# A v cast behind its masks and attention rows ahead of a gate selection, in one TensorE-bound kernel

## The chip, the cores and the metric

The kernel runs on one core of a Trainium2 chip. The metric is the time of one execution on the device in microseconds; lower is better. The core has five engines with an instruction queue each: TensorE (PE in the profile, its weight loads PEld), VectorE (DVE), ScalarE (ACT), GpSimd (POOL) and SyncE (SP), which here only issues transfers. Each engine takes its instructions in the order in which they were written, and waits where an operand or a buffer isn't ready.

## What is computed

The reference is a block-sparse attention followed by a Fourier mixing layer with a small feed-forward network. Cut to what matters:

```
# q, k, v: batch 4, heads 8, seq 768, head dim 64; blocks of 64 keys, 12 of them
gate = einsum(q, mean of k over each block)      # per query and block; future blocks -1e9
sel  = top 3 blocks of the gate, and the query's own block
attn = softmax(where(sel and causal, q k^T / 8, -1e9))
x    = attn @ v                                  # heads side by side: 4 x 768 x 512
u    = x + real(fft(fft(x, axis=seq), axis=model))
un   = (u - mean(u)) / sqrt(var(u) + 1e-6)
out  = u + relu(un @ w_ch1) @ w_ch2              # 512 -> 2048 -> 512
```

## The kernel before

The heads are taken in pairs, four pairs to a batch, so there are 16 pairs, numbered from 0. The whole program is one list of steps written out by hand, ORDER (L115). Each entry is a step's name and its arguments; WORK (L862) says which function it calls. A step appends its instructions to the queues of the engines that it uses, so an engine's order is the order of ORDER restricted to the steps that use it. There is no planner.

The steps that play a part here, P being a pair, i one of six score tiles, b a batch:

- Gate: g:P (TensorE, L414) gate scores in PSUM; gt:P (VectorE, L431) turns them into gt; gx:P (L445) takes the largest eight of each row; gl:P,0 sets the own block's entry and gl:P,1 (L453) compares gt with the third largest, which writes lt: this comparison is a VectorE operation on two SBUF tensors; gm:P (L472) turns lt back into the mask mt. qs:P (GpSimd, L404) copies the queries q32 as float16 into qk, kh:P (GpSimd, L368) is a small product with the block means.
- Scores: s:P,i (TensorE, L487), e:P,i (ScalarE exponential into pt, L515), d:P,i (GpSimd, L523), the causal mask on the diagonal of tile i.
- Values: vc:P (GpSimd, L316) casts the loaded v (nat) to float16 in v16, one of four buffers; v:P (TensorE, L529) is 42 matmuls av that need every tile pt of the pair, its masks, and v16; x:P (VectorE, L542) is a reciprocal rcp of the row sums and one multiplication of av, in PSUM, that writes the rows x of the pair. It also frees the PSUM bank of av.
- Fourier mixing of a batch: fs and fd (VectorE folds of x, L556 and L566, each on two SBUF tensors), f (four more folds, fg), fc (GpSimd, four edge copies, the tile mid among them), y (TensorE), ty:b,0 (ScalarE) and ty:b,1 (here VectorE) copy it out of PSUM, tr:b,0 and tr:b,1 (VectorE, L626) write it reversed, m (TensorE, L632, mx in the profile) is the second transform, u (VectorE, L682) adds x, nm and xu (ScalarE) scale the rows, xt (TensorE) and un (VectorE) turn them.
- Feed-forward: w and r, then c and o; W and X load the weights through GpSimd's queue.

PSUM is handed out in four slots in an order written out by hand as well (PLACES, L187). A slot is given to a new tile only when the last reader of its old tile is done: so the scores s:3,3 take the slot of the av of pair 1, which x:1 empties.

The two places are these. At about 32 us VectorE has the half gl:4,1 of pair 4's selection and behind it x:1, while TensorE works on pair 3's scores. At about 48 us GpSimd has vc:4 (the fifth pair's cast), then the masks d:4,1, the product kh:6, and the masks d:4,4 and d:5,0; behind them qs:6. At that time VectorE does ty:0,1, tr:0,0, tr:0,1 and the sums u of batch 0, and TensorE the steps m of batch 0, then v:4.

Of the kernel before, what the change touches and what calls it, by code (L numbers as in the profile page):

```python
# [120 lines left out]
d:0,1 v:0 ks:3 kh:4 kc:4 Lq:5 kh:3 kc:3 s:1,3 x:0 qs:3 tq:4 e:1,3 d:1,4 s:2,2 d:1,2 qc:4 d:1,3 g:3  # L121
e:2,2 fs:0,1 s:1,5 s:2,1 gt:3 vc:1 e:1,5 s:2,5 Lv:2 e:2,1 g:4 gx:3 qs:4 s:2,0 gl:3,0 e:2,5 gl:3,1
d:1,5 e:2,0 tk:5 gt:4 d:1,1 Lv:3 d:2,2 gx:4 s:2,3 LT:0 d:1,0 s:2,4 Lq:6 gm:3 e:2,3 d:2,5 d:2,1 ks:5
tq:5 e:2,4 v:1 qc:5 kh:5 d:2,0 kc:5 d:2,3 Lk:6 gl:4,0 fs:0,0 s:3,2 gl:4,1 qs:5 x:1 s:3,4 e:3,2 g:5
d:2,4 vc:2 e:3,4 gt:5 s:3,3 s:3,0 gx:5 vc:3 LF:0 e:3,0 s:3,5 v:2 gm:4 fs:1,0 e:3,5 gl:5,0 d:3,4
e:3,3 gl:5,1 d:3,5 s:3,1 x:2 d:3,2 Lv:4 s:4,1 d:3,0 e:3,1 s:4,2 d:3,3 Lq:7 fs:2,0 s:4,3 e:4,1 fs:2,1
gm:5 d:3,1 v:3 W:1 fs:1,1 e:4,3 fd:2,1 fd:2,0 s:4,5 e:4,2 s:5,2 x:3 e:5,2 s:4,0 fs:3,1 s:5,0 fs:3,0
e:4,5 s:5,1 fd:3,1 e:4,0 tk:6 fd:3,0 fc:0 e:5,0 f:0,1 s:4,4 f:0,0 Lk:8 e:5,1 ks:6 y:0,0,0 d:4,5
e:4,4 d:4,0 y:0,0,1 f:0,2 f:0,3 y:0,1,0 d:4,2 ty:0,0 y:0,1,1 d:5,2 d:4,3 kc:6 s:5,3 ty:0,1 d:5,1
s:5,4 W:0 e:5,3 m:0,0 tr:0,0 tr:0,1 e:5,4 m:0,2 vc:4 u:0,0 u:0,1 nm:0,0,1 d:4,1 s:5,5 xu:0,0 m:0,1  # L130
kh:6 u:0,4 d:4,4 nm:0,1,1 e:5,5 d:5,0 u:0,5 nm:0,4,1 xt:0,0 xu:0,1 tq:6 Lk:7 u:0,2 nm:0,5,1 xu:0,4
xt:0,1 u:0,3 v:4 nm:0,2,1 xu:0,5 qc:6 xu:0,2 xt:0,4 un:0,0 xt:0,5 nm:0,3,1 qs:6 xu:0,3 g:6 un:0,2
d:5,4 xt:0,2 xt:0,3 W:2 gt:6 w:0,6,2 w:0,6,0 un:0,1 d:5,3 w:0,5,2 d:5,5 gx:6 w:0,5,0 w:0,5,1 gl:6,0
gl:6,1 gm:6 w:0,6,1 r:0,5 x:4 w:0,3 r:0,6 Lv:5 s:6,3 r:0,3 Lq:8 s:6,2 e:6,3 s:6,4 tq:7 s:6,1 e:6,4
# [780 lines left out]
```

## Time and profile before

| what | value |
|---|---|
| median of 3 runs | 283.35 us (283.18 to 283.54) |
| profiled execution | 283.3 us |
| its span, first to last instruction | 281.6 us |
| TensorE, VectorE, ScalarE, GpSimd busy | 97%, 67%, 60%, 44% of the span |
| granted TensorE clock | 1.00 throughout |

A row of a timeline has the start in microseconds from the start of the span, the length, the engine, the line of the kernel, the operation, what it writes and reads (out<-in, without buffer numbers), their sizes, and how many alike were merged into the row; in brackets stands how long the engine sat idle ahead of it and who ended that. A row of the waits has the waiting instruction, whom it waited for, the sum, the count and the longest. A row by stretches has the bounds, the length, then the busy time and the instruction count of PE, PEld, DVE, ACT and POOL, the granted clock, and the share and rate of the DMA engines. A row of a tile's instructions has the count, the shortest, median and longest duration in ns, and the first and last start in us. Lines such as L246 and L249 are helpers that several steps share, so steps are told apart by their tiles.

### The profile page before, as it was taken

How to read it: one execution, taken by the hardware profiler on the slowest of the kernel's cores; microseconds unless marked ns; L12 is line 12 of the kernel's file. 1: busy time of each engine (PE TensorE's matmuls, PEld its weight loads, DVE VectorE, ACT ScalarE, POOL GpSimd, SP SyncE). 2: the span in 40 equal slices, each digit the busy share in tenths (PEclk: the TensorE clock that was granted, in tenths of full speed). 3: DMA queues.
4: the chain of work that ended last, by engine and by line, in shares of the span. 5: the costliest groups of instructions: out<-in, count | busy, mean ns of one | idle time of the engine just before them, and what ended most of it. 6: DMA issues, size and time to landing. Idle time of an engine off the chain costs nothing. (4 is left out here: it accounts for less than half of the span.)

```text
span 281.6 us, 6726 instructions
## 1 busy us (share of the span) xinstructions
PE 272.2 (97%) x2577; PEld 168.8 (60%) x2577; DVE 187.5 (67%) x570; ACT 168.3 (60%) x230; POOL 122.9 (44%) x318
## 2 busy tenths in 40 slices
PE   7899899999999999999999999999999999999995
PEld 3666676776556655565666654566676545665544
DVE  2888998997977888998379875862184463514114
ACT  3698799769694396595735789659651631353000
POOL 2258748314796459636803873855602020002000
PEclk9999999999999999999999999999999999999999
DMA  8999999997789998749895084440000352400104
GB/s 177 237 210 214 253 171 180 188 165 125 133 115 190 168 123 176 143 87 233 183 150 99 3 249 102 116 134 3 0 3 0 136 147 56 151 0 0 40 37 149
DMA packets 120020, 35.55 MB, mean 126 GB/s; under 512 B 110834, under 2 KB 116018, under 8 KB 119988
## 3 DMA queue, kind: packets, MB, share of 16 engines
q1 hardware_dynamic: 114260, 29.48, 52.6%
q0 software_dynamic: 3984, 5.24, 11.2%
q10 hardware_dynamic: 1744, 0.40, 0.8%
q8 instruction: 20, 0.33, 0.5%
q14 instruction: 12, 0.10, 0.1%
HBM read 29.60 MB, written 7.34 MB: 131 GB/s over the span
## 5 line engine op out<-in xcount | busy, mean ns | idle before, releaser
L520 ACT ACTIVATE pt<-sc 128x1024 f16<-128x1024 f32 (+1 forms) x96 | 82.9, 934 | 24.4 <-PE sc L503 19.7
L756 PE MATMUL h<-unT,w 128*128 128x256 f16 (+1 forms) x528 | 87.0, 321 | 0.0
L781 PE MATMUL c<-w_sb,hT 128*128 128x512 f16 x368 | 83.2, 379 | 0.0
L756 PEld LDWEIGHTS <-w 128*128 128x128 f16 x528 | 51.0, 98 | 31.3
L781 PEld LDWEIGHTS <-hT 128*128 128x128 f16 x368 | 35.7, 98 | 40.7 <-issue 0.5
L766 ACT ACTIVATE hT<-h 128x768 f16<-128x768 f32 x48 | 37.7, 819 | 36.1 <-PE h L756 36.1
L526 POOL TENSOR_SCALAR_AFFINE_SELECT pt<-pt 128x256 f16<-128x256 f16 x96 | 37.6, 416 | 23.8 <-ACT pt L520 22.4
L764 DVE TENSOR_SCALAR hT<-h 128x768 f16<-128x768 f32 x16 | 15.1, 947 | 28.2 <-PE h L756 28.2
L793 DVE SCALAR_TENSOR_TENSOR u<-c,rs,u 128x512 f32<-128x512 f32 (+2 forms) x26 | 17.7, 701 | 24.0 <-PE c L781 22.7
L249 POOL TENSOR_SCALAR_AFFINE_SELECT qk<-q 64x768 f16<-64x768 f32 (+1 forms) x25 | 20.8, 831 | 19.1 <-DVE q L402 7.3
L249 POOL TENSOR_SCALAR_AFFINE_SELECT qk<-mt 32x160 f16<-32x160 f16 x72 | 23.0, 340 | 10.1 <-DVE mt L475 6.9
L503 PE MATMUL sc<-qk 96*128 96x512 f16 (+3 forms) x144 | 26.7, 306 | 0.0
L538 PEld LDWEIGHTS <-pt 128*128 128x128 f16 x672 | 22.2, 97 | 2.7 <-issue 0.7
L538 PE MATMUL av<-v,pt 128*128 128x65 f16 x672 | 23.2, 193 | 0.5 <-POOL v L249 0.4
L503 PEld LDWEIGHTS <-qk 96*128 96x128 f16 x144 | 12.8, 98 | 8.1 <-issue 0.5
L246 POOL TENSOR_TENSOR t<-vr,rs 128x6 f32<-128x6 f32 x12 | 2.6, 218 | 32.1 <-DVE rs L732 31.4
L701 ACT ACTIVATE x<-u,nm 128x512 f16<-128x512 f32 x24 | 16.4, 714 | 0.3
L721 DVE BATCH_NORM_STATS2 bst<-u 128x6 f32<-128x512 f32 x24 | 16.2, 677 | 0.1
L498 PE MATMUL sc<-qk 64*128 64x512 f16 (+3 forms) x112 | 14.8, 306 | 1.4 <-DVE x L246 0.8
L246 DVE TENSOR_TENSOR x<-av,rcp 128x768 f16<-128x768 f32 x16 | 15.3, 958 | 0.5
L687 DVE SCALAR_TENSOR_TENSOR u<-mx,x 128x512 f32<-128x512 f32 x20 | 12.8, 678 | 3.4 <-DMA out_dram<-u 2.2
L387 ACT CAST qk<-k 64x768 f16<-64x768 f32 x18 | 14.9, 828 | 0.2
(112 smaller groups left out, 319.6 us busy)
## 6 DMA issues: line engine op xcount, KB each, us to landing
nat<-in_v_dram SPq DMA_DIRECT2D x16, 384.0 KB, 4.9
out_dram<-u SPq DMA_DIRECT2D x23, 256.0 KB, 2.1
nat<-in_k_dram SPq DMA_DIRECT2D x38, 96.0 KB, 4.1
nat<-in_q_dram SPq DMA_DIRECT2D x38, 96.0 KB, 3.8
nat<-in_k_dram SPq DMA_DIRECT2D x12, 192.0 KB, 4.3
nat<-in_q_dram SPq DMA_DIRECT2D x12, 192.0 KB, 4.5
w_sb<-in_moe_w_ch_dram POOLq DMA_DIRECT2D x2, 1024.0 KB, 11.7
w<-in_moe_w_ch_dram POOLq DMA_DIRECT2D x2, 768.0 KB, 7.3
```

Source lines behind the costliest of these rows:

```text
L246: (eng or nc.vector).tensor_tensor(out=out, in0=in0, in1=in1, op=op)
L249: nc.gpsimd.affine_select(out=out, in_=in_, pattern=[[0, i] for i in n], base=0, channel_multiplier=0, compare_op=ALU.is_ge, fill=0.0)
L503: nc.tensor.matmul(ps[:, e, co:co + q1 - q0], qk[0:96, e, 1, 128 * jt:128 * jt + 128], qk[0:96, e, 0, q0:q1], start=True, stop=True)
L520: nc.scalar.activation(out=d["pt"][:, o:o + 2 * n].rearrange("p (e c) -> p e c", e=2), in_=d["sc", i][:, :, 0:n], func=AF.Exp, scale=0.125)
L526: nc.gpsimd.affine_select(out=dg, in_=dg, pattern=[[0, 2], [1, 128]], base=0, channel_multiplier=-1, compare_op=ALU.is_ge, fill=0.0)
L538: nc.tensor.matmul(av[:, e, 66 * st:66 * st + 65], pt[:, co:co + 128], vv[:, e, jt, 0:65], start=(cnt == 0), stop=(cnt == 20))
L701: nc.scalar.activation(out=x_t[b][:, kt, :], in_=u_t[b, kp][:, k2, :], func=AF.Identity, scale=0.0625, bias=u_t[b, kp, "m"][:, k2:k2 + 1])
L721: nc.vector.bn_stats(out=bst, in_=u_t[b, kt // 2][:, kt % 2, :])
L756: nc.tensor.matmul(hp[:, l:r], w1s, unT[:, dt, l:r], start=(dt == 0), stop=(dt == NDT - 1))
L766: nc.scalar.activation(out=hT, in_=hp, func=AF.Relu)
L781: nc.tensor.matmul(c_ps[b, g[0]][:, st - g[0], :], h_t[b, it][:, 128 * st:128 * (st + 1)], w2_t[0][:, it, :], start=(it == 0), stop=(it == ...
L793: nc.vector.scalar_tensor_tensor(out=o, in0=ps, scalar=st_t[b][1][:, st:st + 1], in1=o, op0=ALU.mult, op1=ALU.add)
```

## The change

Two entries of ORDER stand elsewhere; the work is the same. x:1 stands ahead of gl:4,1, so that VectorE does the reciprocal and the rows of the second pair first and the comparison for the fifth pair's gate after them; GpSimd's qs:5, which stood between the two, follows both and is on another engine. vc:4 stands behind d:5,0 and ahead of u:0,5, so that GpSimd does d:4,1, kh:6, d:4,4 and d:5,0 first. The other changed line is only broken elsewhere.

```
-tq:5 e:2,4 v:1 qc:5 kh:5 d:2,0 kc:5 d:2,3 Lk:6 gl:4,0 fs:0,0 s:3,2 gl:4,1 qs:5 x:1 s:3,4 e:3,2 g:5
+tq:5 e:2,4 v:1 qc:5 kh:5 d:2,0 kc:5 d:2,3 Lk:6 gl:4,0 fs:0,0 s:3,2 x:1 gl:4,1 qs:5 s:3,4 e:3,2 g:5
...
-s:5,4 W:0 e:5,3 m:0,0 tr:0,0 tr:0,1 e:5,4 m:0,2 vc:4 u:0,0 u:0,1 nm:0,0,1 d:4,1 s:5,5 xu:0,0 m:0,1
-kh:6 u:0,4 d:4,4 nm:0,1,1 e:5,5 d:5,0 u:0,5 nm:0,4,1 xt:0,0 xu:0,1 tq:6 Lk:7 u:0,2 nm:0,5,1 xu:0,4
+s:5,4 W:0 e:5,3 m:0,0 tr:0,0 tr:0,1 e:5,4 m:0,2 u:0,0 u:0,1 nm:0,0,1 d:4,1 s:5,5 xu:0,0 m:0,1 kh:6
+u:0,4 d:4,4 nm:0,1,1 e:5,5 d:5,0 vc:4 u:0,5 nm:0,4,1 xt:0,0 xu:0,1 tq:6 Lk:7 u:0,2 nm:0,5,1 xu:0,4
```

## The prediction

> **What bounds the kernel now.** I read the page first, then busy time by stretches, then TensorE's own waits, then the timelines around the two moved steps. Both clocks of the argument are in the profile of one execution: 283.3 us, of which 281.6 are the span, so 1.7 us lie around it; the median of the runs is 283.35, that is 0.05 more.
>
> ```profile
> span 281.6 us, 6726 instructions
> PE 272.2 (97%) x2577; PEld 168.8 (60%) x2577; DVE 187.5 (67%) x570; ACT 168.3 (60%) x230; POOL 122.9 (44%) x318
> PE 21%; DVE 0%; issue 0%
> ...
> 30.00:50.00 20.00, 17.81 (x323) 13.25 (x321) 18.49 (x46) 18.16 (x22) 14.07 (x30) 1.00 1.12 197
> 50.00:220.00 170.00, 169.37 (x1577) 106.50 (x1578) 125.57 (x391) 113.34 (x155) 90.22 (x231) 1.00 0.66 119
> ...
> PE sc L498 <- DVE x L246: 0.8, 1, 0.8
> PE mx L641 <- DVE tr L629: 0.7, 1, 0.7
> PE av L538 <- POOL v L249: 0.4, 1, 0.4
> PE yp L608 <- POOL mid L594: 0.2, 1, 0.2
> ```
>
> TensorE is busy 97% of the span at a granted clock of 1.00. The chain that ended last is TensorE alone and reaches back only through the last 21%, so it says nothing about the middle; the two stretches do. From 50 to 220 us the first column after the length, TensorE, is busy 169.37 of 170.00 us: whatever reaches 50 us earlier can end earlier, as nothing there waits for a fixed time. From 30 to 50 us it is busy 17.81 of 20.00, and VectorE (18.49) and ScalarE (18.16) are as full. The waits name the holes: 0.8 us for attention rows x and 0.7 us for the turned tile tr lie in that stretch. These are the two places that the change touches.
>
> **The second pair's rows, x:1.** It goes from behind gl:4,1 (the second half of a gate selection, one comparison into lt) to ahead of it. Nothing is added or removed, and no DMA is passed on any queue.
>
> ```profile
> 30.44 1.44 PE L538 MATMUL av<-v,pt 128*128 128x65 f16 x42
> 32.73 0.69 PE L421 MATMUL g<-q,kr 128*32 128x288 f32 x8
> 34.24 0.39 PE L498 MATMUL sc<-qk 64*128 64x384 f16 x4 [0.81 <-DVE x L246]
> 44.18 0.76 PE L608 MATMUL yp<-fs_sb,fg 128*128 128x193 f16 x7 [0.20 <-POOL mid L594]
> ...
> 32.16 0.89 DVE L246 TENSOR_TENSOR lt<-gt,mx 128x108 f16<-128x108 f32 x1
> 32.97 0.22 DVE L549 RECIPROCAL rcp<-av 128x12 f32<-128x12 f32 x1
> 33.22 0.96 DVE L246 TENSOR_TENSOR x<-av,rcp 128x768 f16<-128x768 f32 x1
> 34.09 0.47 DVE L435 STREAM_TRANSPOSE gt<-g 128x288 f32<-128x288 f32 x1
> 36.15 0.27 DVE L246 TENSOR_TENSOR lt<-gt,mx 128x108 f16<-128x108 f32 x1
> 36.70 0.23 DVE L549 RECIPROCAL rcp<-av 128x12 f32<-128x12 f32 x1 [0.28 <-PE av L538]
> 44.87 1.22 DVE L246 TENSOR_TENSOR fg<-zw 128x762 f16<-128x762 f16 x2
> ...
> 36.70:46.09 9.39, 8.75 (x155) 6.90 (x154) 9.18 (x19) 9.39 (x12) 5.75 (x14) 1.00 1.11 175
> ...
> 31.98 0.94 POOL L249 TENSOR_SCALAR_AFFINE_SELECT qk<-q 128x768 f16<-128x768 f32 x1
> 33.27 1.75 POOL L249 TENSOR_SCALAR_AFFINE_SELECT v<-nat 128x768 f16<-128x768 f32 x2
> 36.59 1.48 POOL L526 TENSOR_SCALAR_AFFINE_SELECT pt<-pt 128x256 f16<-128x256 f16 x4 [1.21 <-ACT pt L520]
> ...
> 32.52 1.94 ACT L520 ACTIVATE pt<-sc 128x1024 f16<-128x1024 f32 x2 [0.52 <-PE sc L510]
> 35.22 10.74 ACT L520 ACTIVATE pt<-sc 128x1024 f16<-128x1024 f32 x13 [0.76 <-PE sc L510]
> ```
>
> The comparison takes 0.27 us at 36.15 and 0.89 us at 32.16, where it ends 0.13 us behind GpSimd's 0.94 us copy of the queries: it stood still while that copy ran. The rows x took their 0.96 us at 33.22 beside GpSimd's casts of v, so they don't stand still. Their input av was ready at 30.44 + 1.44 = 31.88, before the comparison began. So x:1 can take the comparison's place: reciprocal at 32.16, rows at 32.41, end 33.37 in place of 34.18, a shift of 0.81. TensorE's scores at 34.24 wait for the PSUM bank that x empties; the matmuls ahead of them end at 32.73 + 0.69 = 33.42, so almost all of the 0.81 us hole closes.
>
> That is not yet the gain, since the stretch that follows is VectorE's: 9.18 us busy of 9.39 from 36.70 to the last fold at 46.09, in order, and TensorE waits for its folds at 44.18. What arrives there early waits there longer. VectorE's own list begins with gt at 34.09, behind both steps. The comparison, now last, comes up at 32.41 + (34.09 - 33.22) = 33.28, just when the first cast of v begins (33.27). If it stands still until that cast ends, half of 1.75 us later, and ends 0.13 us after, it is done at 34.27 and gt starts some 0.1 us later than now. But behind it VectorE idled 0.28 us at 36.70, for the av of the third pair, which TensorE now delivers early. Net: 0.28 - 0.10, some 0.2 us gained. One bound: the comparison slips in before the cast, gt starts at about 33.5, and x:2 is held only by TensorE, whose last scores ahead of av need a bank that ScalarE's two exponentials free at 32.52 + 1.94 = 34.46; with some 0.2 us of scores and 1.44 for av x:2 can start near 36.2, a gain of 0.5. The other bound: ScalarE, idle 0.76 us at 35.22 for scores, runs that much earlier, so GpSimd's four selects of 36.59 begin at about 35.8 and may stop two VectorE operations between two SBUF tensors there, a select of 0.37 each: 2 x 0.37 - 0.2, a loss of 0.55. I take a gain of 0.2, because the 0.28 us idle row is the nearest measurement of slack on VectorE.
>
> **The fifth pair's v cast, vc:4.** On GpSimd it goes from ahead of d:4,1, kh:6, d:4,4 and d:5,0 (three masks and a small product) to behind them. The queue keeps its work and passes no DMA: W:0 is issued ahead, as before, and qs:6 comes last.
>
> ```profile
> 47.82 0.91 POOL L249 TENSOR_SCALAR_AFFINE_SELECT v<-nat 128x768 f16<-128x768 f32 x1
> 48.68 0.41 POOL L526 TENSOR_SCALAR_AFFINE_SELECT pt<-pt 128x256 f16<-128x256 f16 x1
> 49.05 0.23 POOL L246 TENSOR_TENSOR kr<-kr,half 128x24 f32<-128x24 f32 x1
> 49.24 1.00 POOL L526 TENSOR_SCALAR_AFFINE_SELECT pt<-pt 128x256 f16<-128x256 f16 x2
> 54.59 0.83 POOL L249 TENSOR_SCALAR_AFFINE_SELECT qk<-q 128x768 f16<-128x768 f32 x1 [4.34 <-DVE q L402]
> ...
> 47.88 2.11 DVE L629 COPY tr<-ty 128x768 f16<-128x768 f16 x2
> L629 DVE COPY tr<-ty x2: 553/1094/1635, 47.9 to 49.4; 128x768 f16<-128x768 f16 x2
> L629 DVE COPY tr<-ty x2: 362/362/363, 98.7 to 99.8; 128x768 f16<-128x768 f16 x2
> 49.91 0.68 DVE L687 SCALAR_TENSOR_TENSOR u<-mx,x 128x512 f32<-128x512 f32 x1
> ...
> 48.60 0.27 PE L642 MATMUL mx<-fd_sb,ty 128*128 128x256 f16 x1
> 49.57 0.28 PE L641 MATMUL mx<-fd_sb,tr 128*128 128x256 f16 x1 [0.70 <-DVE tr L629]
> 50.05 0.28 PE L641 MATMUL mx<-fd_sb,tr 128*128 128x256 f16 x1
> 53.00 1.45 PE L538 MATMUL av<-v,pt 128*128 128x65 f16 x42
> ```
>
> The third row of the second part is the next batch: a copy tr takes 362 ns there. Here the first took 1635 ns and the second 553. The first started at 47.88, just behind the cast, stood through the cast, a mask and the product, and ended at 47.88 + 1.64 = 49.51, 0.27 us after the next mask began (49.24); the second ended at 49.99. TensorE lost 0.70 us at 49.57 and again until 50.05, and VectorE's sums u could only start at 49.91.
>
> From the starts above, GpSimd's steps are 0.86 us apart for the cast, 0.37 for a mask, 0.19 for the product. The new queue is then d:4,1 at 47.82, kh:6 at 48.19, d:4,4 at 48.38, d:5,0 at 48.75, vc:4 from 49.12 to 49.98. The first tr again starts at 47.88. I let it be passed over until the product has gone, as in the row: it ends at 48.38 + 0.27 = 48.65. The mask d:4,4 is held up meanwhile (the two last masks took 1.00 us, against 0.41 + 0.37, so about 0.11 each) and makes way at 48.38 + 0.11 + 0.37 = 48.86; the second tr, 0.25 us later like its row, ends at 49.11. Against 49.99 that is 0.88 us. TensorE is free for it: its eighth ty matmul starts at 48.60. VectorE's u, which starts beside GpSimd in both orders and took its 0.68 us there, moves up by the same amount.
>
> Bounds. If tr gets in behind the first mask it ends at 48.19 + 0.27 = 48.46 and the second around 48.76; TensorE then bounds it: the ty matmuls give way at 48.71, the first two of tr take 0.22, so the row of 50.05 comes at 48.93, a gain of 1.12. If it is passed over three times, as often as now when the cast is counted, it ends at 48.75 + 0.27 = 49.02, and the second behind d:5,0 at about 49.5: a gain of 0.49. I take 0.88, as it follows the row's own step, the product. The cast itself is hidden: it ends at 49.98, v:4 needs it at 53.00 less what is gained, some 52.0, and d:4,1 to d:5,0, now early, have no one waiting. Without those 2 us each microsecond of delay would be one of TensorE's.
>
> The Trainium skill, on the page "SBUF — State Buffer", section "SBUF: two separate sides", calls the access that VectorE and GpSimd share an exclusive lock: who starts first keeps it for its whole instruction, and the other one blocks. Read strictly it lets the copy in after one instruction, and the sum would then be 283.3 - 1.12 - 0.2 = 282.0; the 1635 ns row disagrees, since the copy there outlasted three. The same rule speaks against the other move, as it puts the comparison against the cast of v at 33.27 for the whole cast.
>
> **Sum.** 283.3 - 0.88 - 0.2 = 282.2 for the profiled execution, 282.3 with the 0.05 to the median.
>
> **The rivals.** First, x:1 gives nothing back to the end, or takes a little, because VectorE meets the earlier selects in one place (0.37 - 0.2, so 0.2 lost): 283.35 - 0.88 + 0.2 = 282.7. For it: TensorE's early arrival can only wait at 44.18. Against: the 0.28 us idle is there to be used.
> Second, absorbed later: TensorE has waited 0.4 us for a v cast behind 50 us (the third wait above); if GpSimd or a transfer there doesn't move up with the rest, TensorE waits longer at it and about 283.2 is left. For it: that wait itself; against: it is the only one in 170 us.
> Third, slower: VectorE doesn't get in at all while GpSimd has another instruction ready. The new run from 47.82 to 49.98 is unbroken; then the first tr ends near 50.25, the second near 50.6, 0.6 late; likewise the comparison at 33.28 stands through both casts until 35.02 and ends at 35.15, so gt is 1.0 late, 0.7 behind the idle time. 283.35 + 0.6 + 0.7 = 284.7. It decides from the point where the second tr ends past 49.99. Against: tr got in at 49.24 and the comparison at 32.92 between instructions that followed each other.
> Fourth, the 1635 ns don't come from GpSimd at all, and the move changes nothing there: 283.1, x:1 alone.
>
> **How the numbers follow.** A change of under 0.2%, 0.57 us, can't be told from none here. The forecast, both parts paying, has 0.65, from 281.7 (1.12 + 0.5) to 282.8; 0.62 of it lies beyond 0.2%. The first rival has 0.14, its time just faster: 0.09 faster, 0.05 within. The second has 0.09, within. The third 0.08, slower. The fourth 0.04, within. That makes 0.71 faster, 0.21 within, 0.08 slower. The range goes from 281.7 to 283.4, the sum of the worst ends of both parts (0.49 gained, 0.55 lost), and leaves out the third rival and some of the tails.
>
> **What would show it.** Right: x ends at 33.4, the scores behind it without a wait; lt at about 33.3 takes near 1 us; x:2's reciprocal starts at 36.5; in the mx stage, counted from the start of GpSimd's W:0, the first tr ends 1.6 us later, not 2.5, and TensorE's 0.70 us wait shrinks below 0.2. Wrong: a tr over 1.6 us, an lt over 1.7 us, a longer TensorE wait for folds at 44 us that eats everything, or a new wait past 50 us.

## The result

The changed kernel takes 283.82 us (median of 22 runs), the kernel before 283.24 us beside it (22 runs): a ratio of 1.0024, with a 95% interval from 1.0016 to 1.0033. It is slower by about 0.6 us, where some 1.1 us less (0.88 and 0.2) was forecast, and lies above the range.

TensorE's waits in the changed kernel, by the waiting line, its releaser, the sum in us, the count and the longest:

```profile
span 282.8 us, 6727 instructions
...
PE mx L641 <- DVE tr L629: 1.3, 1, 1.3
PE tp L346 <- DMA nat<-in_q_dram: 0.6, 1, 0.6
PE tp L350 <- DMA nat<-in_k_dram: 0.6, 1, 0.6
PE yp L608 <- POOL mid L594: 0.6, 1, 0.6
PE av L538 <- POOL v L249: 0.4, 1, 0.4
PE sc L498 <- DVE x L246: 0.4, 2, 0.2
PE av L538 <- DVE gt L436: 0.2, 1, 0.2
```

The 0.8 us ahead of the scores is gone, as forecast. In its place stand two waits for x and one for gt of some 0.2 us each, and the wait for the folds (mid) grew from 0.2 to 0.6. The wait for tr, which was to shrink below 0.2, grew from 0.7 to 1.3. Behind that stage no new wait came; the 0.4 us for a cast of v stands there as before.

The same timelines as in the prediction, now of the changed kernel:

```profile
32.33 0.45 DVE L246 TENSOR_TENSOR sd<-x 128x384 f16<-128x384 f16 x1
32.96 0.96 DVE L246 TENSOR_TENSOR x<-av,rcp 128x768 f16<-128x768 f32 x1
33.83 0.97 DVE L246 TENSOR_TENSOR lt<-gt,mx 128x108 f16<-128x108 f32 x1
34.91 0.48 DVE L435 STREAM_TRANSPOSE gt<-g 128x288 f32<-128x288 f32 x1
37.25 0.22 DVE L549 RECIPROCAL rcp<-av 128x12 f32<-128x12 f32 x1
38.50 0.83 DVE L246 TENSOR_TENSOR sd<-x 128x384 f16<-128x384 f16 x2
...
33.79 1.78 POOL L249 TENSOR_SCALAR_AFFINE_SELECT v<-nat 128x768 f16<-128x768 f32 x2
38.64 0.49 POOL L526 TENSOR_SCALAR_AFFINE_SELECT pt<-pt 128x256 f16<-128x256 f16 x1 [0.68 <-ACT pt L520]
47.77 0.79 POOL L848 DMA_DIRECT2D w<-in_moe_w_ch_dram  x1
48.58 0.42 POOL L526 TENSOR_SCALAR_AFFINE_SELECT pt<-pt 128x256 f16<-128x256 f16 x1
48.95 0.24 POOL L246 TENSOR_TENSOR kr<-kr,half 128x24 f32<-128x24 f32 x1
49.15 0.90 POOL L526 TENSOR_SCALAR_AFFINE_SELECT pt<-pt 128x256 f16<-128x256 f16 x2
50.01 0.89 POOL L249 TENSOR_SCALAR_AFFINE_SELECT v<-nat 128x768 f16<-128x768 f32 x1
...
L629 DVE COPY tr<-ty x2: 799/1284/1770, 48.6 to 49.3; 128x768 f16<-128x768 f16 x2
```

Part of the 1.2 us between the two spans is not the change's. The first row, a fold sd ahead of both moved steps, starts at 32.33 against 31.79 before: this execution was 0.54 us late before it reached them, after waits for the first transfers of q and k. That start differs from one execution to the next (30.8 to 32.3 us in the profiles of this document). So the stretches are compared from marks within each execution: from that sd row to the start of GpSimd's W:0 (the weight load at 47.77) for x:1, and from there to the end of the span for vc:4. The marks of the kernel before are these two rows:

```profile
31.79 0.45 DVE L246 TENSOR_TENSOR sd<-x 128x384 f16<-128x384 f16 x1
47.02 0.79 POOL L848 DMA_DIRECT2D w<-in_moe_w_ch_dram  x1
```

| kernel | sd | W:0 | span | sd to W:0 | W:0 to end |
|---|---|---|---|---|---|
| before | 31.79 | 47.02 | 281.6 | 15.23 | 234.6 |
| changed | 32.33 | 47.77 | 282.8 | 15.44 | 235.0 |

By these marks x:1 cost 0.2 us and vc:4 0.4 us. Together that is the 0.6 us of the medians. Each is read from one execution; the table behind the experiments shows how well such marks repeat.

### The profile page after: what moved, and what is told of

It reads as the page before. It is cut to its first block, busy times and chain, and to the rows that moved or that the text cites. A ratio compares the mean times of both kernels' runs of the same rounds, so it can differ in the third digit from the quotient of the medians.

```text
span 282.8 us, 6727 instructions
## 1 busy us (share of the span) xinstructions
PE 272.7 (96%) x2577; PEld 169.2 (60%) x2577; DVE 188.3 (67%) x570; ACT 168.2 (60%) x230; POOL 123.3 (44%) x318
```

## The experiments

The theory at this point: VectorE operations that stand still beside GpSimd explain both parts. The second copy tr is kept out by the whole rest of GpSimd's run, the cast at its end included, and the comparison and a fold take back what x:1 won. The rivals: all of it is x:1's; it is the early transfers; the copies tr are slow for another reason than GpSimd. Each row of the table at the end of this section comes from the profile of the kernel named. Four kernels (tail_short, product_last, tail_product and cast_twice) ran once only, so nothing is read from their times.

**The cast alone** (cast_only):

```
-... m:0,2 vc:4 u:0,0 u:0,1 nm:0,0,1 d:4,1 ... kh:6 u:0,4 d:4,4 ... d:5,0 u:0,5
+... m:0,2 u:0,0 u:0,1 nm:0,0,1 d:4,1 ... kh:6 u:0,4 d:4,4 ... d:5,0 vc:4 u:0,5
```

> Only vc:4 is moved, x:1 stands as before. Theory (the copies tr are kept out while GpSimd's instructions follow each other without a gap, so the cast at the end of the run prolongs the wait): the second tr again outlasts the cast, 1.6 to 1.8 us, ends some 3.3 us behind the start of W:0 in place of 2.97 before, TensorE waits about 1.2 us for tr, and the time is 0.3 to 0.5 us over before. Rival one (the loss comes from x:1 ahead of the gate selection, and the cast is neutral or gains): within 0.2 us of before, or up to 0.9 us under it. Rival two (the loss is the transfers at 10 us, which came later in the profile of the changed kernel): no difference to before beyond the noise.

Its ratio to before is 0.9997 (0.9981 to 1.0013), medians 283.52 and 283.34: the interval holds both a loss of 0.36 us and none. The profile is sharper; the instructions on tr, with shortest, median and longest duration in ns:

```profile
L629 DVE COPY tr<-ty x2: 792/1280/1768, 48.2 to 48.9; 128x768 f16<-128x768 f16 x2
...
PE mx L641 <- DVE tr L629: 1.3, 1, 1.3
PE sc L498 <- DVE x L246: 0.8, 1, 0.8
PE yp L608 <- POOL mid L594: 0.2, 1, 0.2
```

The copies are those of the changed kernel, and W:0 to the end takes 234.9, 0.3 to 0.4 us over before, with x:1 in its old place. So rival one falls, and so does the one of the transfers. This rests on the marks, as the medians can't decide it.

**The rows alone** (rows_only):

```
-... gl:4,0 fs:0,0 s:3,2 gl:4,1 qs:5 x:1 s:3,4
+... gl:4,0 fs:0,0 s:3,2 x:1 gl:4,1 qs:5 s:3,4
```

> Only x:1 is moved, vc:4 stands as before. Theory (the comparison stands still beside the cast of v, and one fold meets a mask that comes earlier; VectorE gives all of TensorE's early arrival back): TensorE's 0.81 us wait ahead of the scores is gone, the folds fd end at the same time or 0.2 us later against before, counted from the same start, and the time is 0 to 0.25 us over before. Rival one (all of the loss is x:1's): 0.5 to 0.6 us over before. Rival from the prediction (x:1 gains): 0.2 us under before.

Ratio 1.0001 (0.9986 to 1.0016), medians 283.51 and 283.34. The marks: sd to W:0 takes 15.43, 0.20 us over before, and W:0 to the end is unchanged.

```profile
L246 DVE TENSOR_TENSOR lt<-gt,mx x2: 329/650/971, 33.1 to 36.3; 128x108 f16<-128x108 f32 x2
31.60 0.44 DVE L246 TENSOR_TENSOR sd<-x 128x384 f16<-128x384 f16 x1
36.51 0.22 DVE L549 RECIPROCAL rcp<-av 128x12 f32<-128x12 f32 x1
37.76 0.83 DVE L246 TENSOR_TENSOR sd<-x 128x384 f16<-128x384 f16 x2
```

From sd to the reciprocal of x:2 it takes 4.91 us, as before (36.70 - 31.79): the idle 0.28 us is eaten. The two folds behind x:2 then take 0.83 us in place of 0.63. That is the loss. The mask d:3,1 now starts 6.30 us behind sd, beside the first of the two folds, where it started 6.63 us behind sd, beside the second; these are the fold and the mask of the kernel before, then the mask of rows_only:

```profile
37.96 0.63 DVE L246 TENSOR_TENSOR sd<-x 128x384 f16<-128x384 f16 x2
38.42 0.43 POOL L526 TENSOR_SCALAR_AFFINE_SELECT pt<-pt 128x256 f16<-128x256 f16 x1 [0.35 <-ACT pt L520]
```
```profile
37.90 0.48 POOL L526 TENSOR_SCALAR_AFFINE_SELECT pt<-pt 128x256 f16<-128x256 f16 x1 [0.69 <-ACT pt L520]
```

**The rows alone, with the casts out of the comparison's way** (rows_clear):

```
-... v:1 qc:5 kh:5 ... s:3,2 gl:4,1 qs:5 x:1 s:3,4 ... d:2,4 vc:2 e:3,4 ... gx:5 vc:3 LF:0 ... gl:5,0 d:3,4
+... v:1 qc:5 vc:2 kh:5 ... s:3,2 x:1 gl:4,1 qs:5 s:3,4 ... d:2,4 e:3,4 ... gx:5 LF:0 ... gl:5,0 d:3,4 vc:3
```

> x:1 moved alone, and the casts of the third and fourth pair taken from beside the comparison: vc:2 ahead of kh:5 (about 30 us), vc:3 behind d:3,4 (about 35 us). Theory (x:1 gains nothing because the comparison stands still beside vc:2, and because VectorE's folds meet GpSimd later): the comparison takes 0.27 to 0.35 us in place of 0.97, gt starts about 0.6 us earlier, part of it is lost at a fold beside vc:3, and TensorE's wait for the folds at 44 us falls from 0.58 to 0.1 to 0.4 us; time 0.1 to 0.5 us under x:1 moved alone. Rival (something else sets the folds, for instance TensorE's av of the third pair): the comparison is short and the folds end when they did.

The comparison takes 260 ns now, and sd to W:0 15.08: 0.35 us under the rows alone and 0.15 under before.

```profile
L246 DVE TENSOR_TENSOR lt<-gt,mx x2: 260/295/330, 33.4 to 36.2; 128x108 f16<-128x108 f32 x2
35.43 0.72 DVE L246 TENSOR_TENSOR sd<-x 128x384 f16<-128x384 f16 x1
PE yp L608 <- POOL mid L594: 0.6, 1, 0.6
```

So the cast beside the comparison is what kept x:1 from paying: from sd to the reciprocal of x:2 it now takes 4.57 us (36.46 - 31.89) in place of 4.91, while the two folds behind it still take 0.83. Half of what the short comparison frees is taken again at once: a fold at 35.43 now takes 0.72 us beside vc:3. No run moves the two casts and leaves x:1 in its old place, so how much of the 0.15 us is x:1's own isn't shown. That TensorE's wait for the folds would shrink was wrong; it stays at 0.6, since TensorE comes early by as much. In time the ratio to before is 0.9998 (0.9989 to 1.0007), which tells the 0.15 us from nothing no better.

**The cast out of the run** (cast_early), in GpSimd's idle time behind W:1:

```
-... v:3 W:1 fs:1,1 ... m:0,2 vc:4 u:0,0
+... v:3 W:1 vc:4 fs:1,1 ... m:0,2 u:0,0
```

> The kernel before with vc:4 taken out of the crowded run altogether: it stands behind W:1, where GpSimd idles until the edge copies at 43 us. Theory: the run at 48 us has one instruction less, the first tr ends at about 1.65 us behind the start of W:0 and the second behind d:5,0, at about 2.4 us in place of 2.97; TensorE's wait shrinks from 0.70 to about 0.2 us, and the time is 0.4 to 0.7 us under before. Rival (the copies are slow for another reason than GpSimd's queue): the same time as before within 0.2 us, tr still over 1.5 us.

```profile
L629 DVE COPY tr<-ty x2: 554/670/786, 48.3 to 49.0; 128x768 f16<-128x768 f16 x2
48.20 0.42 POOL L526 TENSOR_SCALAR_AFFINE_SELECT pt<-pt 128x256 f16<-128x256 f16 x1
48.57 0.24 POOL L246 TENSOR_TENSOR kr<-kr,half 128x24 f32<-128x24 f32 x1
48.77 1.01 POOL L526 TENSOR_SCALAR_AFFINE_SELECT pt<-pt 128x256 f16<-128x256 f16 x2
```

The second copy, which in the changed kernel is passed over by d:5,0 and the cast, gets in ahead of d:5,0 here: 554 ns, as before. It was expected to get in behind d:5,0 and end 2.4 us behind the start of W:0, and ends 2.11 us behind it; TensorE's wait for tr, expected at 0.2, is gone from the list. W:0 to the end takes 233.7, 0.9 us under before; the ratio is 0.9981 (0.9968 to 0.9995), medians 282.84 and 283.34.

**GpSimd held until both copies are done** (after_hold), on the changed kernel:

```
-... tr:0,0 tr:0,1 e:5,4
+... tr:0,0 tr:0,1 hp:0 e:5,4
...
+    held = ctile([128, 1], F16, "held")
...
+    def hold(b):
+        pcopy(held, ys[b, 1, 1][:, 0, 0:1], [1])
```

> The changed kernel, with one GpSimd copy of a single column of the second tr placed ahead of d:4,1, so that GpSimd waits until both copies are done and then does its run. Theory: both tr take 0.36 us, the second ends 1.5 us behind the start of W:0, TensorE's wait for tr is under 0.1 us, GpSimd's run ends with the cast at about 51 us, still ahead of v:4, and the time is 1.2 to 1.7 us under the changed kernel, 0.6 to 1.1 us under before. Rival (the copies are slow for another reason): tr stays over 1.5 us and the time is not under the changed kernel; rival (later waits take it back): tr is short but the time falls by less than 0.5 us.

```profile
L630 DVE COPY tr<-ty x2: 343/350/356, 47.7 to 47.9; 128x768 f16<-128x768 f16 x2
46.84 0.79 POOL L852 DMA_DIRECT2D w<-in_moe_w_ch_dram  x1
48.39 0.18 POOL L249 TENSOR_SCALAR_AFFINE_SELECT held<-tr 128x1 f16<-128x1 f16 x1 [0.76 <-DVE tr L630]
49.80 0.89 POOL L249 TENSOR_SCALAR_AFFINE_SELECT v<-nat 128x768 f16<-128x768 f32 x1
53.42 0.83 POOL L249 TENSOR_SCALAR_AFFINE_SELECT qk<-q 128x768 f16<-128x768 f32 x1 [2.72 <-DVE q L403]
```

With GpSimd idle for 0.76 us both copies take 0.35 us, and TensorE's wait for tr is gone from the list. The time is 282.04 against 283.34, a ratio of 0.9950 (0.9931 to 0.9968). W:0 to the end takes 233.5. This settles it: the copies are slow because of GpSimd's run, and nothing behind takes the gain back. The time fell by more than expected, 1.30 us where 0.6 to 1.1 was forecast. The marks say why: they give 1.1 gained behind W:0 and 0.2 lost to x:1, and the other 0.4 lies ahead of the first mark (sd starts at 31.41 against 31.79), where the hold does nothing yet. In the five kernels that have its extra tile held, sd starts at 30.80 to 31.43, in the nine others at 31.42 to 32.33; whether the tile does that is open.

**What keeps the second copy out.** Four kernels vary what stands behind it in GpSimd's queue; x:1 stands as before in all of them. tail_short is the early cast with a copy of one column behind d:5,0; in product_last the run is d:4,1, d:4,4, d:5,0, kh:6, vc:4; tail_product is the early cast with the run d:4,1, d:4,4, d:5,0, kh:6; cast_twice does the cast early and once more behind d:5,0.

```
tail_short    +... d:5,0 hp:0 u:0,5          (hp copies a column of id16)
product_last  +... m:0,1 u:0,4 d:4,4 ... d:5,0 kh:6 vc:4 u:0,5
tail_product  +... W:1 vc:4 fs:1,1 ... m:0,1 u:0,4 d:4,4 ... d:5,0 kh:6 u:0,5
cast_twice    +... W:1 vc:4 fs:1,1 ... d:5,0 vc:4 u:0,5
```

The expectations, in that order:

> Like the kernel with the early cast (run of d:4,1, kh:6, d:4,4, d:5,0), with one GpSimd copy of a single column behind d:5,0, so that d:5,0 is no longer the last instruction that is ready. Theory A (a waiting copy gets in ahead of the last ready instruction of the run, and an instruction more behind it keeps the copy out, whatever its length): the second tr is passed over by d:5,0 as in the changed kernel and ends behind it, 2.3 to 2.6 us behind the start of W:0, with a duration of 0.75 to 1.0 us. Theory B (only the long cast is special): 0.55 us and 2.12 us, as with the early cast.

> Like vc:4 moved alone, with kh:6 between d:5,0 and vc:4, so the run is d:4,1, d:4,4, d:5,0, kh:6, vc:4. Theory A (a copy gets in behind the small product): the first tr is passed over by all three masks and kh:6 and ends 2.3 to 2.5 us behind the start of W:0 (duration 1.4 to 1.7 us), and the second behind the cast, at about 3.4 us. Theory B (a copy gets in behind the second instruction that passes it, whichever that is): the first tr ends at about 1.8 us (duration 0.9 to 1.0).

> As with the early cast, but kh:6 stands behind d:5,0, so the run is d:4,1, d:4,4, d:5,0, kh:6. If a follower behind d:5,0 that itself waits for another engine's semaphore is what keeps the second tr out, the first tr ends 1.44 us behind the start of W:0 and the second is passed over by d:5,0 and kh:6 and ends at 2.4 to 2.6 us. If only the cast behind them does it, the second ends at 1.9 to 2.0 us.

> vc:4 is done early and once more behind d:5,0, so the second cast waits for no transfer any more. If the length of the follower keeps the second tr out, or that it is a cast, the second tr ends behind it, at 3.3 us behind the start of W:0, as in the changed kernel. If its wait for the transfer did, the second tr gets in ahead of d:5,0 and ends at 2.12 us. The work is that of the kernel with the early cast and one cast more.

The rows on tr, again in that order:

```profile
L630 DVE COPY tr<-ty x2: 554/675/796, 48.7 to 49.4; 128x768 f16<-128x768 f16 x2
```
```profile
L629 DVE COPY tr<-ty x2: 592/1283/1974, 47.5 to 48.0; 128x768 f16<-128x768 f16 x2
```
```profile
L629 DVE COPY tr<-ty x2: 554/574/593, 48.4 to 48.9; 128x768 f16<-128x768 f16 x2
```
```profile
L629 DVE COPY tr<-ty x2: 800/1285/1770, 48.2 to 49.0; 128x768 f16<-128x768 f16 x2
```

The one-column follower doesn't keep the second copy out (554), nor does the product, which depends on VectorE's sums kr (554). The cast does, also when it waits for no transfer (1770), and also from two places further back (1974). So theory A of the short tail fell, and so did a wait as the reason. The first copy fits neither theory of product_last: there a mask stands next and it got in at once (592), where the product stands next it is passed over. What sets this order I can't say. That a cast which stands behind holds the second copy out until it is through is shown in four kernels (the changed one, cast_only, product_last, cast_twice), and that the second copy gets in at the next change of instruction without one in six. This is no rule for every operation. The first copy was passed over by a mask and the product in the kernel before, with no cast behind them (1635 ns), and the comparison of the changed kernel got in between two casts that followed each other: it ended at 34.80, while the second cast ran until 35.57. Whether it is the cast's length or its kind that holds the copy out wasn't tried.

**Holding without the other moves.** early_hold has the early cast, cast_hold the cast at the end of the run; both have the hold, and x:1 as before. after_hold2 repeats after_hold beside cast_hold.

```
early_hold  +... W:1 vc:4 fs:1,1 ... tr:0,0 tr:0,1 hp:0 e:5,4 ...
cast_hold   +... tr:0,0 tr:0,1 hp:0 e:5,4 ... d:5,0 vc:4 u:0,5
```

> The kernel before with vc:4 in GpSimd's idle time at 40 us and the single-column copy that holds GpSimd until the second tr is done; x:1 stands as before. Theory (the wait for tr is all that is to be had there, and x:1's move costs 0.2 us): tr 0.36 us each, TensorE waits under 0.1 us for tr, the scores at 34 us wait 0.8 us as before, time 1.1 to 1.6 us under before, so up to 0.3 us under the changed kernel with the hold. Rival (x:1's move gains something once tr is quick): slower than the changed kernel with the hold, by 0.2 us or more.

> vc:4 moved as in the change, x:1 as before, and the single-column copy that holds GpSimd until the second tr is done. If x:1's move costs 0.2 us, as the traces say, this is 0.1 to 0.3 us under the changed kernel with the hold in the same call; if x:1's move gains, it is over it. Against before: 1.1 to 1.6 us under. Unlike the early cast with the hold, no cast stands beside the folds at 40 us, so its times should lie close together.

> The changed kernel with the hold once more, as the neighbour of the kernel with the hold and without x:1's move: 0.9 to 1.4 us under before, 0.1 to 0.3 us over that neighbour.

early_hold: 281.75 us against 283.10, ratio 0.9962 (0.9948 to 0.9976), but its runs spread from 281.2 to 283.1. cast_hold: 281.90 against 283.43, ratio 0.9946 (0.9928 to 0.9965). after_hold2: 282.01 against the same 283.43, ratio 0.9953 (0.9936 to 0.9969). The medians put x:1's move at 0.1 us, too little to tell; the marks put it at 0.2 again. cast_hold beats both the kernel before and the changed one, and is what I would keep: the cast behind the masks, the rows where they were, and GpSimd held back. By the marks its gain is 1.1 us; the rest of the medians' 1.5 must lie ahead of sd, as in after_hold.

| kernel | x:1 first | sd | W:0 | span | sd to W:0 | W:0 to end |
|---|---|---|---|---|---|---|
| rows_only | yes | 31.60 | 47.03 | 281.6 | 15.43 | 234.6 |
| rows_clear | yes | 31.89 | 46.97 | 281.5 | 15.08 | 234.5 |
| cast_only | no | 32.13 | 47.36 | 282.3 | 15.23 | 234.9 |
| cast_early | no | 31.94 | 47.40 | 281.1 | 15.46 | 233.7 |
| tail_short | no | 31.19 | 47.88 | 281.6 | 16.69 | 233.7 |
| product_last | no | 31.42 | 46.65 | 281.5 | 15.23 | 234.9 |
| tail_product | no | 31.60 | 47.53 | 281.0 | 15.93 | 233.5 |
| cast_twice | no | 31.59 | 47.39 | 282.3 | 15.80 | 234.9 |
| after_hold | yes | 31.41 | 46.84 | 280.3 | 15.43 | 233.5 |
| after_hold2 | yes | 31.43 | 46.86 | 280.4 | 15.43 | 233.5 |
| cast_hold | no | 31.07 | 46.29 | 279.8 | 15.22 | 233.5 |
| early_hold | no | 30.80 | 46.24 | 279.7 | 15.44 | 233.5 |

The marks repeat closely. Without an early cast and with the casts vc:2 and vc:3 in their old places, the first stretch takes 15.22 or 15.23 us in the four kernels with x:1 in its old place, and 15.43 or 15.44 in the four with x:1 first. The second takes 234.9 to 235.0 wherever the second copy waits for a cast, and 233.5 wherever GpSimd is held.

In cast_early the first stretch is 0.2 us longer with x:1 in its old place. Its trace shows where: the early cast runs beside two later folds sd, which take 0.85 us at 41.47 where they take 0.63 at 41.32 in the kernel before.

## Why the prediction was wrong, point by point

**What bounds the kernel** was right: TensorE's holes between 30 and 50 us set the time, everything behind moved with them: from W:0 to the end it takes 233.5 us with the hold, 234.6 before and 235.0 changed. The second rival, absorbed later, was wrong.

**x:1's own move** was right in its first half. The rows came at the comparison's place (32.96, that is 32.42 less the late start, forecast 32.41), the comparison stood through the cast (0.97 us) and TensorE's hole closed. The failed step is "Net: 0.28 - 0.10". The comparison ended where the forecast had it (34.80 less 0.54 is 34.26, forecast 34.27). But gt, from 34.09 to 34.91 less 0.54, came 0.28 us later and not 0.1: it started 0.11 us behind the comparison's end, where it had started 0.09 us before the end of the rows x. The kernel gives the reason: gt has a single buffer (bufs=1 in g_turn), which the comparison reads, so the next gt can't be written before the comparison is done, while x leaves that buffer alone; no run gave gt a second buffer, so this is read from the kernel and the rows. The later gt ate the idle time. Then a fold behind x:2 met the mask d:3,1, which ScalarE's earlier exponential had brought forward, and 0.2 us were lost. The first rival comes nearest, with one select met and 0.2 us lost, but its price is right by luck: it set a select of 0.37 against a gain of 0.2, where the gain was nothing and the fold lost 0.2, and it meant the four selects of 36.59, while the one met was the next, d:3,1. It had 0.14, and took the sum for vc:4 as given.

**vc:4's move** failed at one step: "makes way at 48.86; the second tr, 0.25 us later like its row, ends at 49.11", 2.09 us behind the start of W:0. The first copy did as forecast: 799 ns, done 1.65 us behind W:0, forecast 1.63. The second got in nowhere; it outlasted d:4,4, d:5,0 and the cast and ended 3.34 us behind W:0, against 2.97 before. I had read from one row (553 ns) that a waiting copy gets in at the next change of instruction. That row had no cast behind it. Moving the cast to the end of the run is what put one there. The lower bound, three instructions passed over and 0.49 us gained, came from the first copy's row, and let the second be passed over only once. The other bound, TensorE's own pace with 1.12 us gained, is what the hold brought: from 234.6 to 233.5 us behind W:0.

**The third rival** is right for one operation of three. The second copy was kept out to the end of the run, at the place and from the point named: it decides "where the second tr ends past 49.99". But as a rule, that VectorE doesn't get in while GpSimd has another instruction ready, it fell: the first copy and the comparison got in between instructions that followed each other, and so did the second copy wherever no cast stood behind it. Its price of 1.3 us was too high for that reason: only the second copy was kept out, and it cost 0.4 us. The prediction had cited a rule from the Trainium skill, page "SBUF — State Buffer", section "SBUF: two separate sides", that who starts first keeps the shared access for its whole instruction. The 1770 ns row of this case goes further than that sentence: the copy had asked before d:5,0 and the cast started, and both went first.

**The cover** of the cast held: it ended at 50.90 and no one waited for it. **The range** had its upper end at the worst of both ends, a loss of 0.06 us; that the second copy ends later than before was missing from it.

## What to carry to other kernels

Where VectorE's operation is slow beside GpSimd, count how long GpSimd's queue stays full behind it, and with what, not only which instruction stands next to it; moving a long instruction to the end of that run can make it worse, as the cast did for the second copy here. If GpSimd has time left (2.7 us here), let it wait for VectorE with a cheap dependent instruction: that gave 1.1 us by the marks, 0.4%. One reordering, tail_product, got as much behind W:0 in its one execution, but its early cast cost 0.7 us ahead of it. Before an instruction is moved, look too for what reuses the buffer that it reads. A step that closes a hole on the bounding engine pays only if the engine that feeds it next also moves up. Marks within one execution tell 0.2 us where medians don't, and they show what part of a gain lies outside the change.

## What was not expected

In one execution the hold of a ready GpSimd cast reached over a transfer issue as well. With the early cast behind W:1, in the kernel with the short tail, the cast didn't wait for its transfer, and the fold zw that started beside the issue of W:1 stood through it and the cast: 2.01 us of the 2.48 for two. In the profile of cast_early the cast still waited 0.80 us for its transfer, and the folds beside W:1 took their 0.55 us. The rows, first of tail_short, then of cast_early:

```profile
38.53 2.48 DVE L246 TENSOR_TENSOR zw<-sd 128x768 f16<-128x768 f16 x2
38.20 0.99 POOL L852 DMA_DIRECT2D w<-in_moe_w_ch_dram  x1
39.21 0.91 POOL L249 TENSOR_SCALAR_AFFINE_SELECT v<-nat 128x768 f16<-128x768 f32 x1
```
```profile
39.17 0.99 POOL L848 DMA_DIRECT2D w<-in_moe_w_ch_dram  x1 [0.17 <-issue]
40.95 0.90 POOL L249 TENSOR_SCALAR_AFFINE_SELECT v<-nat 128x768 f16<-128x768 f32 x1 [0.80 <-DMA nat<-in_v_dram]
```

So the price of the early cast depends on where it lands among VectorE's folds, and that changes with its transfer. Over the five kernels that have it, the stretch from sd to W:0 takes 15.44 to 16.69 us, against 15.23 before. Each time the excess is that of the folds beside the cast: 0.85 us for two sd in cast_early against 0.63 before, 0.84 in early_hold and 1.32 in tail_product; 1.60 for two zw in cast_twice against 1.03; and 2.48 in tail_short against 1.01. That may be why the early cast with the hold spreads over almost 2 us; none of its longer executions was profiled, so this is not shown.
